# First token product of batch 1 in three round-format products, V rows for pairs 2 and 3, and a new list of the attention phase

## The chip, the cores and the metric

One core of a Trainium2 chip runs the whole program. The metric is the device time of one execution in microseconds (us), the median of the runs shown. Before the change it is 558.04 us (three runs, 557.51 to 558.55).

## The reference, cut to what matters

The program computes three blocks in a row on two batches of 768 rows and 512 columns.

```python
# attention: 8 heads of 64 columns, blocks of 32 rows, a window of 16
k_sum = k.reshape(B, H, nb, block, D).max(axis=3)
v_sum = v.reshape(B, H, nb, block, D).mean(axis=3)
scores = [local scores inside the window | scores on k_sum + log(block)]
x = softmax(scores) @ [v | v_sum]            # becomes (B, 768, 512)
# first mixer: across the rows (tokens), then across the columns (channels)
xt = x.transpose(0, 2, 1)
h = relu(xt @ w_tok1) @ w_tok2               # w_tok1 is 768 x 256
u = x + h.transpose(0, 2, 1)
y = u + relu(u @ w_ch1) @ w_ch2
# second mixer: normalised rows, channels only
out = y + relu(norm(y) * g @ moe2_w_ch1) @ moe2_w_ch2
```

## The kernel before, in words

**Two phases.** The first is the attention phase: attention of both batches, both token products of batch 0 and the first token product of batch 1. The order of every engine's instructions in it is written out by hand in the list FRONT: each word is a letter (what is done, by the table `do` in `attention`) and a number (which piece). The words are issued in that order on all engines, so each engine works through its own words strictly in turn, and waits where a word isn't ready. The second phase is the channel products, about 464 us of them, ordered by the planner and, later, by the program.

**Attention.** Two heads make a pair; pairs 0 to 3 are batch 0, 4 to 7 are batch 1. A pair has three groups n (n = 3 * pair, + 1, + 2), so there are 24. Each group goes through q (scores, TensorE, 16 small products), m (mask and minimum, VectorE), e (exponential, ScalarE), t (four transposes, TensorE), c (copy out, ScalarE), a (product with V, TensorE) and n (division by the row sum, VectorE), which writes the group into `u`. Keys, queries and V have three buffers each, by pair modulo 3, so a pair's loads wait for the last use of the pair three before.

**V.** There are two ways to get a pair's V in rows. Pairs below NT come transposed with their neighbours (v loads 552 KB into a wide tile), get their block means on VectorE or GpSimd (s or p, and S or T), and are turned by TensorE: w is four transposes, and x or X copies them out by ScalarE or VectorE. The other pairs load V rows ready from memory (r, 780 KB) and V transposed (v, 384 KB); GpSimd makes the means (s), TensorE turns them once (S, one transpose), ScalarE copies them out (z), and GpSimd writes them into the rows (u). NT is 4.

**Token products.** The weights arrive as 64-bit words in halves of 128 x 512 (h loads one, W and D decode it). Halves 0 to 2 are `w_tok1`. `g1(b, hf, t)` is a piece of the first token product: six F32 products of 128 x 256 accumulate over the six row tiles of a batch, then ScalarE makes the high half of the result (hh) and VectorE the low half (hl). There are eight pieces, four for each batch: g0 to g3 for batch 0, g10, g11, g20 and g21 for batch 1. `g2` is the second token product (six pieces g4 to g9 for batch 0); there each operand is split into a high half in the round format (F32R) and the rest, and `mm3` makes three products: high by high, high by low, low by high. C splits off the high half of a weight half (ScalarE), O the low half (VectorE). P, or g12 to g19, transpose `u` of batch 0 for the second phase.

**f** is a product of zeros on TensorE that nothing reads.

**Around the change.** The first token product of batch 1 needs all of `u` of batch 1, so its pieces g20 and g21 stand at the end of the list. The second phase's first product follows the last transposes.

Of the kernel before, what the change touches and what calls it, by code (L numbers as in the profile page):

```python
# [11 lines left out]
F32 = mybir.dt.float32  # L12
# [32 lines left out]
EARLY = 16  # L45
NEG = -8e9
EPS = 1e-9
NT = 4
FRONT = """
d0 f d1 f j0 f f j1 f f i0 v0 f i1 f l1 f K0 f v1 q0 l2 f f m0 f f e0 f h1 q1 t0 m1 f c0 f q2  # L50
e1 f m2 f l3 e2 t1 s0 f f f v2 t2 k1 S0 h2 w1 v3 w0 K1 x1 h0 q3 X0 c1 w2 m3 p1 a0 e3 q4 n0 c2 t3 m4
x2 a1 e4 k2 q5 T1 a2 n1 K2 c3 w3 m5 W1 t4 x3 D1 q6 c4 a3 e5 n2 w5 m6 w4 x5 t5 x4 n3 q7 p2 c5 k3 a4
e6 m7 a5 e7 t6 n4 r4 q8 n5 J3 S2 p3 t7 c6 m8 h4 w7 W2 y2 w6 X7 c7 q9 l4 e8 X6 a7 D2 v4 a6 S3 W0 v5
n7 w11 l5 w9 m9 x11 t8 x9 w8 D0 c8 q10 x8 w10 n6 e9 g1 X10 W4 k4 D4 K4 s4 t9 m10 C4 g0 c9 O4 G1 e10
H1 s5 q11 G0 H0 t10 l6 m11 S4 a8 e11 k5 q12 h3 z4 t11 c10 h7 n8 u4 a9 h5 m12 v7 e12 a10 n9 r5 J5 q13
n10 c11 t12 m13 a11 c12 k6 e13 q14 S5 a12 J6 m14 z5 e14 u5 t13 n12 q15 n11 c13 t14 W3 m15 a13 W7 D3
q16 e15 g2 m16 e16 s7 n13 D7 C3 c14 t15 O3 C7 q17 c15 t16 m17 G2 a14 e17 H2 q18 n14 r7 c16 a15 m18
e18 a16 l7 n15 q19 n16 W5 g3 h6 D5 v6 h8 m19 C5 h9 e19 r6 O5 t17 t18 G3 c17 q20 H3 k7 c18 g7 m20 K7
e20 g5 H7 W6 q21 H5 s6 g8 m21 e21 D6 S7 g6 W8 H8 h10 C6 D8 z7 t19 W9 u7 S6 g4 z6 O6 h11 H6 u6 q22 H4
g9 m22 e22 q23 H9 a18 m23 b g19 n18 g12 G19 a17 G12 H19 t20 H12 c19 g13 n17 c20 g16 t21 G16 a19 G13  # L60
H16 e23 a20 H13 n19 g11 c21 n20 t23 G11 g15 H11 t22 G15 g14 c22 H15 a21 G14 g18 c23 n21 a22 G18 H14
a23 n22 g10 n23 H18 g20 G10 H10 g21 G20 H20 P17 G21 G17 H21 H17
"""
SCALE = 1.0 / math.sqrt(D)

# [5 lines left out]
class Kern:  # L71
# [342 lines left out]
    def prep_v2(self, i):  # L414
        nc = self.nc
        if i < NT:
            zs = self.vs.pop(i)
            nc.scalar.activation(
                self.wide[i][:, :, 0:NB],
                zs.rearrange("p (o n) -> p o n", o=1).to_broadcast([P, 7, NB]),  # L420
                AF.Copy,
                scale=1.0 / BLOCK,
            )
            return
        self.psv = self.ps_pt.tile([P, 512], F32, tag="pt", name=f"psv{i}")
        nc.tensor.transpose(self.psv[:NK, 0:P], self.Z[i % 2], self.ident)

    def prep_v3(self, i):
        self.zs = self.att.tile([NK, P], F32, tag="zs", bufs=1, name=f"zs{i}")
        self.nc.scalar.activation(self.zs, self.psv[:NK, 0:P], AF.Copy, scale=1.0 / BLOCK)  # L430

    def prep_v4(self, i):
        nc, src = self.nc, self.zs
        V = self.V[i % 3].rearrange("p (w j) c -> p j w c", j=2)
        for a, j in ((0, 0), (96, 1)):
            out = V[a : a + NB, j, :, 0:130].rearrange("p w (r c) -> p w r c", r=2)[:, :, :, 0:64]
            x = src[a : a + NB].rearrange("p (o r c) -> p o r c", o=1, r=2).to_broadcast([NB, 6, 2, 64])
            nc.gpsimd.tensor_copy(out, x)

    def att_vtr(self, n):  # L440
        i, qd = divmod(n, 3)
        ps = self.ps_mm.tile([P, 512], F32, tag="mm", name=f"vtr{n}")
# [127 lines left out]

    def g1(self, b, hf, t):
        nc = self.nc
        ps = self.ps_mm.tile([P, 512], F32, tag="mm", name=f"g1_{b}_{hf}_{t}")
# [12 lines left out]
        yield  # L586
        nc.vector.scalar_tensor_tensor(hl, ps[:, :256], 0.0, f32(hh), op0=ALU.max, op1=ALU.subtract)
        yield

    def g2(self, b, only=None):  # L590
        nc = self.nc
        for st in range(ST) if only is None else (only,):
            ps = self.ps_mm.tile([P, 512], F32, tag="mm", name=f"g2_{b}_{st}")
# [19 lines left out]
    def transpose_u(self, g, only=None):  # L613
        nc = self.nc
        th, tl = self.new_xt(("u", g))
        for cc in range(CC) if only is None else (only,):
            ps = self.bank or self.ps_mm.tile([P, 512], F32, tag="mm", name=f"tu_{g}_{cc}")
            self.bank = None
            for j in range(GT):
                nc.tensor.transpose(  # L620
# [513 lines left out]
    def attention(self):  # L1134
# [8 lines left out]
        def other_bank(k):  # L1143
# [35 lines left out]
            "C": self.split_hi,  # L1179
            "O": lambda h: [0 for _ in self.split_lo(h)],  # L1180
# [15 lines left out]
    def run(self):  # L1196
# [260 lines left out]
```

## Time and profile before

| | |
|---|---|
| runs shown | 558.04 us median, 557.51 to 558.55 |
| the profiled execution's own time | 557.49 us |
| its span, first to last instruction | 555.7 us |
| TensorE busy | 548.7 us (99%), 3673 instructions |
| VectorE busy | 405.1 us (73%) |
| ScalarE busy | 272.2 us (49%) |
| GpSimd busy | 36.6 us (7%), all in the attention phase |
| memory traffic | 137 MB, 247 GB/s on average |

Busy TensorE is not TensorE at its peak: products are pipelined and their ends are modelled, so where work follows work the time of one is read from start to start. The profiled execution is 0.55 us faster than the median. Some records of products are missing, so counts are taken from the list and the code. The attention phase ends where the first channel product starts, at 91.3 us.

### The profile page before, as it was taken

The page shows a single profiled execution, that of the slowest core. Times are in us where ns is not written, and L with a number is a line of the kernel's source. Part 1 is how long each engine was busy: PE and PEld are TensorE (multiplying, and loading weights), DVE is VectorE, ACT ScalarE, POOL GpSimd, SP SyncE. Part 2 cuts the span into 40 slices and gives each one's busy share as a digit, 9 for nine tenths or more (in the row PEclk, how much of TensorE's full clock was granted, in tenths as well). Part 3 has the DMA queues.
Part 4 walks back from the last instruction along what each step waited for, and adds up shares of the span by engine and source line. Part 5 has one row for each costly group of instructions (what it writes and reads, how often), then busy time and mean ns, then how long its engine had stood idle before and what let it go on. Part 6 is the DMA issues. An engine that isn't in the chain of part 4 may idle for free.

```text
span 555.7 us, 10285 instructions
## 1 busy us (share of the span) xinstructions
PE 548.7 (99%) x3673; PEld 495.0 (89%) x3674; DVE 405.1 (73%) x977; ACT 272.2 (49%) x602; POOL 36.6 (7%) x76
## 2 busy tenths in 40 slices
PE   8999999999999999999999999999999999999997
PEld 4887789898998989989999988988989999999997
DVE  5989874648876887665579957888866776777771
ACT  5979663138755645454787325554422222334320
POOL 7454400000000000000000000000000000000000
PEclk9999999999999999999999999999999999999999
DMA  8876810435788779888656996898787897777455
GB/s 326 313 298 242 327 57 1 151 109 197 248 297 292 266 282 315 283 313 296 230 207 234 317 312 195 284 313 278 257 300 234 292 314 253 240 234 254 162 168 173
DMA packets 55651, 137.00 MB, mean 247 GB/s; under 512 B 5681, under 2 KB 13489, under 8 KB 55601
## 3 DMA queue, kind: packets, MB, share of 16 engines
q1 hardware_dynamic: 55600, 136.36, 71.6%
q8 instruction: 29, 0.48, 0.3%
q14 instruction: 22, 0.17, 0.1%
HBM read 101.73 MB, written 34.60 MB: 245 GB/s over the span
## 4 chain that ended last, share of the span: by engine, by line
PE 91%; ACT 3%; DVE 2%; DMA 2%; POOL 0%; issue 0%; SPq 0%; DVEq 0%; POOLq 0%; ACTq 0%
PE m L319 8%; PE m L318 8%; PE m L317 8%; PE acc_x L318 4%; PE acc_x L319 4%; PE acc_x L317 4%; PE g L575 3%; PE acc_y L319 2%; PE acc_y L318 2%; PE acc_y L317 2%; DMA V<-in_v_dram 2%; ACT pr L519 1%; PE av L547 1%; PE acc_m L319 1%; PE acc_m L318 1%; PE acc_m L317 1%
## 5 line engine op out<-in xcount | busy, mean ns | idle before, releaser
L317 PE MATMUL m<-slot,slot 128*128 128x384 f32 (+1 forms) x136 | 45.8, 337 | 0.0
L319 PE MATMUL m<-slot,slot 128*128 128x384 f32 (+1 forms) x136 | 45.4, 334 | 0.0
L318 PE MATMUL m<-slot,slot 128*128 128x384 f32 (+1 forms) x136 | 45.4, 334 | 0.0
L319 PE MATMUL acc_x<-slot,al 128*128 128x512 f32 x96 | 37.8, 394 | 0.0
L318 PE MATMUL acc_x<-slot,ah 128*128 128x512 f32 x96 | 37.8, 394 | 0.0
L317 PE MATMUL acc_x<-slot,ah 128*128 128x512 f32 x96 | 37.5, 391 | 0.0
L519 ACT ACTIVATE pr<-sn,mn 128x120 f32<-128x120 f32 x96 | 29.7, 389 | 6.6 <-DVE mn L504 6.6
L317 PEld LDWEIGHTS m<-slot,slot 128*128 128x128 f32 x136 | 25.6, 188 | 1.8
L318 PEld LDWEIGHTS m<-slot,slot 128*128 128x128 f32 x136 | 25.6, 188 | 1.6
L165 DVE SCALAR_TENSOR_TENSOR dec<-stage,dec 128x512 uint32<-128x512 uint32 x36 | 25.5, 708 | 0.7
L319 PEld LDWEIGHTS m<-slot,slot 128*128 128x128 f32 x136 | 25.5, 188 | 0.0
L142 ACT ACTIVATE dec<-stage 128x512 f32<-128x512 f32 x36 | 24.2, 676 | 0.1
L871 ACT ACTIVATE ah<-sm 128x384 fp32r<-128x384 f32 x16 | 8.4, 525 | 28.1 <-DVE sm L881 28.1
L575 PE MATMUL g<-u,tok 128*128 128x256 f32 x96 | 22.1, 383 | 0.0
L504 DVE CUSTOM_DVE_ANT_0 sn<-scores,mask 128x120 f32<-128x120 f32 x92 | 20.4, 277 | 2.2 <-PE scores L485 2.1
L703 ACT ACTIVATE f_B<-tx,gt 128x384 f32<-128x384 f32 x16 | 9.3, 582 | 25.4 <-PE tx L699 25.4
L319 PEld LDWEIGHTS acc_x<-slot,al 128*128 128x128 f32 x96 | 18.0, 188 | 4.0
L243 DVE TENSOR_TENSOR slot<-dec,slot 128x512 fp32r<-128x512 f32 x27 | 20.1, 743 | 0.1
L319 PE MATMUL acc_y<-slot,al_s 128*128 128x256 f32 x72 | 20.1, 280 | 0.0
L318 PE MATMUL acc_y<-slot,ah_s 128*128 128x256 f32 x72 | 20.1, 279 | 0.0
L575 PEld LDWEIGHTS g<-u,tok 128*128 128x128 f32 x96 | 17.8, 190 | 2.6 <-issue 0.3
L666 ACT ACTIVATE xn<-u,nb,rs 128x128 f32<-128x128 f32 x48 | 20.1, 483 | 0.0
(1516 smaller groups left out, 1732.5 us busy)
## 6 DMA issues: line engine op xcount, KB each, us to landing
stage<-in_wts_dram SPq DMA_DIRECT2D x62, 512.0 KB, 4.4
slot<-w1s SPq DMA_DIRECT2D x94, 256.0 KB, 3.6
w1s<-sps SPq DMA_DIRECT2D x16, 512.0 KB, 4.4
w2s<-sp SPq DMA_DIRECT2D x16, 512.0 KB, 3.4
slot<-w2s SPq DMA_DIRECT2D x16, 512.0 KB, 4.8
w2t<-wk SPq DMA_DIRECT2D x16, 512.0 KB, 5.0
slot<-w2t SPq DMA_DIRECT2D x8, 768.0 KB, 5.0
slot<-w2s SPq DMA_DIRECT2D x22, 256.0 KB, 4.3
```

The costliest lines, as they stand in the source:

```text
L142: fold = lambda out: nc.scalar.activation(out, high, AF.Prelu, scale=2.0**-112, alpha=-(2.0**32))
L165: put(m, t[:, :, 0], 29, m, op0=ALU.logical_shift_right, op1=ALU.bitwise_or)
L243: (engine or nc.vector).tensor_tensor(wl, x, f32(wh), op=ALU.subtract)
L317: nc.tensor.matmul(out, lhs[0], rhs[0], start=first, stop=False)
L318: nc.tensor.matmul(out, lhs[0], rhs[1], start=False, stop=False)
L319: nc.tensor.matmul(out, lhs[1], rhs[0], start=False, stop=last)
L504: nc.vector.tensor_tensor_reduce(sn[:, u], ps[u % 2][:, u // 2, :NK], self.mask[:, mv], scale=-SCALE, scalar=3e38, op0=ALU.add, op1=ALU.mi ...
L519: self.nc.scalar.activation(self.pr[n][:, u], sn[:, u], AF.Exp, bias=mn[:, u : u + 1], scale=-1.0)
L575: nc.tensor.matmul(ps[:, :256], self.tok1(st, t), self.u[:, b * ST + st, 256 * hf : 256 * hf + 256], start=st == 0, stop=st == ST - 1,)
L666: nc.scalar.activation(xn[:, j], self.u[:, g * GT + j, cc * P : cc * P + P], AF.Identity, bias=nb[:, j : j + 1], scale=rs[:, j : j + 1],)
L703: nc.scalar.activation(x, ps[:, :GN], AF.Copy, scale=self.gt[:, cc : cc + 1])
L871: nc.scalar.activation(ah, x, AF.Relu)
```

## The change

NT goes from 4 to 2, so pairs 2 and 3 get V rows from memory. Batch 1's first token product uses `mm3` on halves: `tok_hi` and `tok_lo` split the three halves of `w_tok1` (C0 to C2, O0 to O2), and `split_u` splits each group of batch 1 as it is ready (U12 to U23 on ScalarE, L12 to L23 on VectorE). The second pair of tiles for the parts takes the place of the third buffers of keys, queries and V, which B closes. The two accumulation banks of the attention phase are held as two fixed tiles used in turn. The list is a new one.

```diff
-NT = 4
+NT = 2
     def tok1(self, st, t):
         col = st * DTOK + t * P
-        return self.half[col // 512][:, col % 512 : col % 512 + P]
+        return self.tok[:, col // 512, col % 512 : col % 512 + P]
+    def tok_hi(self, h):
+        w, e = self.slot(h // 2), 512 * (h % 2)
+        self.half[h] = w[:, e : e + 512], w[:, 1024 + e : 1536 + e]
+        self.nc.scalar.copy(self.half[h][0], self.tok[:, h])
+    def tok_lo(self, h):
+        hi, lo = self.half[h]
+        self.nc.vector.tensor_tensor(lo, self.tok[:, h], f32(hi), op=ALU.subtract)
+    def u_parts(self, hf, qd):
+        return tuple(t[:, 2 * qd : 2 * qd + 2] for t in self.us[hf])
+    def parts_tiles(self, pool, hf):
+        self.us[hf] = [pool.tile([P, ST, 256], F32R, name=f"us{hf}{i}") for i in range(2)]
+    def close_late(self):
+        self.lctx.close()
+        self.parts_tiles(self.actx.enter_context(self.tc.tile_pool(name="parts", bufs=1, side="right")), 1)
+    def split_u(self, n, k):
...
+        hi, lo = (t[:, :, e : e + P] for t in self.u_parts(p // 2, qd))
+        x = self.u[:, b * ST + 2 * qd : b * ST + 2 * qd + 2, p * P : p * P + P]
+        if k == 0:
+            nc.scalar.copy(hi, x)
+        else:
+            nc.vector.tensor_tensor(lo, x, f32(hi), op=ALU.subtract)
+    def mm_bank(self, name):
+        if not self.banks:
+            return self.ps_mm.tile([P, 512], F32, tag="mm", name=name)
+        self.banks.rotate(1)
+        return self.banks[0]
     def g1(self, b, hf, t):
...
+            if b == 1:
+                rhs = tuple(x[:, st % 2] for x in self.u_parts(hf, st // 2))
+                self.mm3(ps[:, :256], self.weight(st // 2, st % 2 * DTOK + t * P), rhs, st == 0, st == ST - 1)
+                continue
```

Counted over the two lists, the words that differ in number are these; q, m, e, t, c, a, n, D, W, h, k and the pieces are as many as before (five more of the eight transposes of `u` are called P instead of g, which gives them a bank of their own).

| word | before | after | engine of one |
|---|---|---|---|
| f | 22 | 2 | TensorE |
| w (four transposes of V) | 12 | 6 | TensorE |
| x, X (copies of these) | 8, 4 | 5, 1 | ScalarE, VectorE |
| S as a copy / as one transpose | 3 / 4 | 0 / 6 | ScalarE / TensorE |
| z, u | 4, 4 | 6, 6 | ScalarE, GpSimd |
| s on VectorE / on GpSimd | 1 / 4 | 1 / 6 | |
| p (means of a wide tile) / T (their copy) | 3 / 1 | 1 / 2 | GpSimd |
| r (load of V rows) | 4 | 6 | DMA |
| B (closes the third buffers) | 0 | 1 | |
| K / J (copy of the key maxima) | 5 / 3 | 7 / 1 | ScalarE / GpSimd |
| C | 5 | 8 | ScalarE |
| O / o (low half of a weight half) | 4 / 0 | 3 / 4 | VectorE / GpSimd |
| U, L | 0, 0 | 12, 12 | ScalarE, VectorE |

The beginning and the end of the two lists:

```
before: d0 f d1 f j0 f f j1 f f i0 v0 f i1 f l1 f K0 f v1 q0 l2 f f m0 f f e0 f h1 q1 t0 m1 f c0 f q2 ...
... t23 G11 g15 H11 t22 G15 g14 c22 H15 a21 G14 g18 c23 n21 a22 G18 H14 a23 n22 g10 n23 H18 g20 G10 H10 g21 G20 H20 P17 G21 G17 H21 H17
after: d0 d1 f j0 j1 v0 l1 i0 v1 i1 l2 K0 q0 h0 v2 q1 m0 e0 f m1 q2 e1 s0 t0 l3 t1 c0 T0 k1 r2 w0 h2 m2 w2 K1 x0 v3 e2 h1 q3 a0 ...
... P12 L16 c22 g8 n21 W9 L17 G12 n20 U18 t23 H8 U20 g11 c23 L19 L18 H12 L20 D8 a23 G11 U21 a22 n23 h10
g10 n22 U23 H11 U22 L23 L21 L22 P16 P18 g20 G18 G10 H10 g21 G20 G16 H20 H16 H18 P17 P19 G17 G19 H17 G21 H21 H19
```

## Rows read from the trace of the kernel before

**Rows 1.** Windows: busy us per engine (instructions), clock, DMA share, GB/s; the second phase.
```profile
91.25:555.70 464.45, 461.21 (x2583) 427.20 (x2581) 333.82 (x674) 209.27 (x431) 0.00 (x0) 1.00 0.74 248
```

**Rows 2.** Windows: the attention phase from its first scores, in four stretches.
```profile
5.40:30.59 25.19, 24.82 (x400) 18.93 (x402) 21.30 (x109) 22.32 (x63) 12.54 (x26) 1.00 0.91 351
30.59:54.10 23.51, 22.79 (x344) 18.32 (x342) 21.72 (x104) 19.88 (x59) 11.92 (x21) 1.00 0.66 249
54.10:71.70 17.60, 16.30 (x146) 12.25 (x142) 15.88 (x54) 10.79 (x31) 7.77 (x14) 1.00 0.80 306
71.70:91.25 19.55, 19.55 (x206) 17.00 (x200) 9.92 (x34) 8.16 (x21) 0.00 (x0) 1.00 0.09 29
```

**Rows 3.** Waits of TensorE that show: who waited for whom, us, times, longest.
```profile
PE g L317 <- DVE u L604: 0.9, 1, 0.9
PE scores L485 <- POOL V L438: 0.5, 1, 0.5
```

**Rows 4.** Timeline of TensorE (start, us, line, operation): start of the program.
```profile
1.25 4.07 PE L1194 MATMUL warm_ps<-warm 128*128 128x512 bf16 x10 [1.25 <-DVE warm L1247]
5.40 0.64 PE L485 MATMUL scores<-K,Q 64*64 64x120 f32 x16
5.98 1.25 PE L1194 MATMUL warm_ps<-warm 128*128 128x512 bf16 x5
```

**Rows 5.** Timeline of TensorE: one of each of the attention phase's pieces.
```profile
30.10 0.65 PE L446 MATMUL vtr<-ident,VW 128*120 128x128 f32 x4
30.59 2.76 PE L575 MATMUL g<-u,tok 128*128 128x256 f32 x12
33.18 0.60 PE L528 MATMUL pt<-ident,pr 128*120 128x128 f32 x4
...
36.30 0.64 PE L485 MATMUL scores<-K,Q 64*64 64x120 f32 x16
36.87 0.65 PE L528 MATMUL pt<-ident,pr 128*120 128x128 f32 x4
37.36 0.27 PE L426 MATMUL psv<-ident,Z 128*120 128x128 f32 x1
37.56 0.69 PE L547 MATMUL av<-V,PT 121*64 121x65 f32 x16
38.18 0.64 PE L485 MATMUL scores<-K,Q 64*64 64x120 f32 x16
...
59.74 0.39 PE L317 MATMUL g<-hh,slot 128*128 128x512 f32 x1
59.97 0.39 PE L318 MATMUL g<-hl,slot 128*128 128x512 f32 x1
```

**Rows 6.** Timeline of TensorE near the end: round-format products of 256 columns.
```profile
536.20 0.28 PE L317 MATMUL acc_m<-slot 128*128 128x256 f32 x1
...
536.56 0.28 PE L317 MATMUL acc_m<-slot 128*128 128x256 f32 x1
```

**Rows 7.** Groups by line: count, busy us, mean ns of one, idle before.
```profile
L230 ACT CAST sp<-dec 128x256 fp32r<-128x256 f32 x8 | 3.2, 403 | 0.0
L222 ACT CAST slot<-dec 128x512 fp32r<-128x512 f32 x27 | 16.6, 614 | 2.1 <-DVE dec L165 2.1
L257 DVE TENSOR_TENSOR sp<-dec,sp 128x256 fp32r<-128x256 f32 x8 | 3.3, 416 | 0.0
L243 DVE TENSOR_TENSOR slot<-dec,slot 128x512 fp32r<-128x512 f32 x27 | 20.1, 743 | 0.1
L453 DVE COPY V<-vtr 120x512 f32<-120x512 f32 x4 | 2.7, 688 | 0.9 <-PE vtr L446 0.9
```

**Rows 8.** Timeline of all engines: VectorE's subtraction beside GpSimd's additions.
```profile
33.71 2.82 POOL L400 TENSOR_TENSOR VT<-VT 128x384 f32<-128x384 f32 x4 [7.90 <-DMA VT<-in_vt_dram]
...
34.12 1.14 DVE L243 TENSOR_TENSOR slot<-dec,slot 128x512 fp32r<-128x512 f32 x1
```

**Rows 9.** DMA issues of the first 92 us: KB each, median us to landing.
```profile
V<-in_v_dram SPq DMA_DIRECT2D x4, 780.0 KB, 7.0
```

More of the change, by code (lines that the diff above doesn't have):

```diff
@@ L47 @@
 EPS = 1e-9
-NT = 4
+NT = 2
 FRONT = """
[L50 to L59, printed above, removed]
@@ L60 @@
-g9 m22 e22 q23 H9 a18 m23 b g19 n18 g12 G19 a17 G12 H19 t20 H12 c19 g13 n17 c20 g16 t21 G16 a19 G13
-H16 e23 a20 H13 n19 g11 c21 n20 t23 G11 g15 H11 t22 G15 g14 c22 H15 a21 G14 g18 c23 n21 a22 G18 H14
-a23 n22 g10 n23 H18 g20 G10 H10 g21 G20 H20 P17 G21 G17 H21 H17
+d0 d1 f j0 j1 v0 l1 i0 v1 i1 l2 K0 q0 h0 v2 q1 m0 e0 f m1 q2 e1 s0 t0 l3 t1 c0 T0 k1 r2 w0 h2 m2 w2
+K1 x0 v3 e2 h1 q3 a0 p1 m3 c1 e3 n0 q4 w1 m4 t2 x1 k2 x2 q5 T1 e4 a1 m5 l4 J2 w3 c2 n1 q6 e5 s2 t3
+m6 w4 e6 X3 q7 a2 m7 c3 t4 x4 n2 q8 c4 k3 W0 S2 w5 e7 a3 m8 a4 D0 K3 t5 z2 x5 u2 q9 c5 n3 h4 t6 e8
@@ new lines @@
+m9 v4 a5 r3 n4 q10 l5 c6 s3 n5 W2 a6 m10 W1 t7 t8 c7 n6 q11 c8 D1 e9 v5 a8 a7 D2 e10 S3 t9 n7 g1 h5
+z3 k4 r4 c9 h3 m11 K4 l6 W4 D4 r5 t10 G1 u3 e11 q12 g0 m12 C0 e12 n8 s4 k5 c10 K5 q13 C4 a9 m13 e13
+t11 o4 v6 n9 t12 q14 H1 c11 s5 G0 a10 m14 W5 l7 a11 c12 n10 q15 n11 t13 S4 H0 g2 z4 D5 c13 v7 u4 e14
+h7 m15 h6 W3 C5 t14 D3 S5 e15 o5 q16 a13 m16 G2 a12 C3 n13 q17 o3 H2 U13 g3 k6 z5 c14 e16 u5 m17 n12
+L13 t15 s6 G3 t16 K6 H3 c15 k7 q18 e17 a15 m18 a14 e18 n15 q19 s7 r7 n14 g7 U15 r6 m19 h8 e19 q20 H7
@@ new lines @@
+U14 t17 m20 K7 g6 C2 c16 O0 W7 L15 t18 L14 C1 q21 D7 c17 a16 e20 a17 m21 h9 S7 g5 H6 z7 U12 u7 c18
+n17 W6 n16 g4 e21 D6 S6 t19 H4 z6 h11 U16 u6 q22 c19 y2 H5 t20 C7 m22 b g15 e22 P13 O2 a19 G15 a18
+O1 G13 q23 H15 c20 n18 g9 W8 H13 U17 C6 n19 g14 H9 o6 B U19 t21 G14 t22 m23 c21 a20 e23 H14 a21 L12
+P12 L16 c22 g8 n21 W9 L17 G12 n20 U18 t23 H8 U20 g11 c23 L19 L18 H12 L20 D8 a23 G11 U21 a22 n23 h10
+g10 n22 U23 H11 U22 L23 L21 L22 P16 P18 g20 G18 G10 H10 g21 G20 G16 H20 H16 H18 P17 P19 G17 G19 H17
@@ L63 @@
+G21 H21 H19
 """
@@ L424, in prep_v2 @@
             return
-        self.psv = self.ps_pt.tile([P, 512], F32, tag="pt", name=f"psv{i}")
-        nc.tensor.transpose(self.psv[:NK, 0:P], self.Z[i % 2], self.ident)
+        self.psv[i] = self.ps_pt.tile([P, 512], F32, tag="pt", name=f"psv{i}")
+        nc.tensor.transpose(self.psv[i][:NK, 0:P], self.Z[i % 2], self.ident)
     def prep_v3(self, i):
-        self.zs = self.att.tile([NK, P], F32, tag="zs", bufs=1, name=f"zs{i}")
-        self.nc.scalar.activation(self.zs, self.psv[:NK, 0:P], AF.Copy, scale=1.0 / BLOCK)
+        self.zs[i] = self.att.tile([NK, P], F32, tag="zs", bufs=1, name=f"zs{i}")
+        self.nc.scalar.activation(self.zs[i], self.psv.pop(i)[:NK, 0:P], AF.Copy, scale=1.0 / BLOCK)
     def prep_v4(self, i):
-        nc, src = self.nc, self.zs
+        nc, src = self.nc, self.zs.pop(i)
         V = self.V[i % 3].rearrange("p (w j) c -> p j w c", j=2)
@@ L441, in att_vtr @@
         i, qd = divmod(n, 3)
-        ps = self.ps_mm.tile([P, 512], F32, tag="mm", name=f"vtr{n}")
+        ps = self.mm_bank(f"vtr{n}")
         for u in range(4):
@@ L572, in g1 @@
         nc = self.nc
-        ps = self.ps_mm.tile([P, 512], F32, tag="mm", name=f"g1_{b}_{hf}_{t}")
+        ps = self.mm_bank(f"g1_{b}_{hf}_{t}")
         for st in range(ST):
+            if b == 1:
+                rhs = tuple(x[:, st % 2] for x in self.u_parts(hf, st // 2))
+                self.mm3(ps[:, :256], self.weight(st // 2, st % 2 * DTOK + t * P), rhs, st == 0, st == ST - 1)
+                continue
             nc.tensor.matmul(
@@ L592, in g2 @@
         for st in range(ST) if only is None else (only,):
-            ps = self.ps_mm.tile([P, 512], F32, tag="mm", name=f"g2_{b}_{st}")
+            ps = self.mm_bank(f"g2_{b}_{st}")
             for t in range(2):
@@ L616, in transpose_u @@
         for cc in range(CC) if only is None else (only,):
-            ps = self.bank or self.ps_mm.tile([P, 512], F32, tag="mm", name=f"tu_{g}_{cc}")
+            ps = self.bank or self.mm_bank(f"tu_{g}_{cc}")
             self.bank = None
@@ L1178, in attention @@
             "b": lambda _: self.close_wide(),
-            "C": self.split_hi,
-            "O": lambda h: [0 for _ in self.split_lo(h)],
+            "C": lambda h: (self.split_hi if h > 2 else self.tok_hi)(h),
+            "O": lambda h: [0 for _ in self.split_lo(h)] if h > 2 else self.tok_lo(h),
+            "B": lambda _: self.close_late(),
+            "U": lambda n: self.split_u(n, 0),
+            "L": lambda n: self.split_u(n, 1),
             "o": lambda h: [0 for _ in self.split_lo(h, nc.gpsimd)],
@@ L1230, in run @@
         att = self.att
-        self.Q = [att.tile([P, S], F32, name=f"Q{i}") for i in range(3)]
-        self.K = [att.tile([P, 7, 184], F32, name=f"K{i}") for i in range(3)]
+        self.us = {}
+        self.parts_tiles(att, 0)
+        self.actx, self.lctx = actx, ExitStack()
+        late = self.lctx.enter_context(tc.tile_pool(name="late", bufs=1, side="right"))
+        at = (att, att, late)
+        self.Q = [at[i].tile([P, S], F32, name=f"Q{i}") for i in range(3)]
+        self.K = [at[i].tile([P, 7, 184], F32, name=f"K{i}") for i in range(3)]
         self.PT = [att.tile([NK + 1, 512], F32, name=f"PT{i}") for i in range(2)]
-        self.V = [att.tile([P, NW, VC], F32, name=f"V{i}") for i in range(3)]
+        self.V = [at[i].tile([P, NW, VC], F32, name=f"V{i}") for i in range(3)]
         self.VT = [att.tile([P, S], F32, name=f"VT{i}") for i in range(2)]
-        self.vs, self.vps, self.sn = {}, {}, {}
+        self.vs, self.vps, self.sn, self.psv, self.zs = {}, {}, {}, {}, {}
         self.Z = [att.tile([P, NK], F32, name=f"Z{i}") for i in range(2)]
@@ L1263, in run @@
         nc.scalar.activation(first, first, AF.Exp)
-        self.wps = self.ps_mm.tile([P, 512], F32, tag="mm", name="warm_ps")
+        self.banks = deque(self.ps_mm.tile([P, 512], F32, tag="mm", name=f"mm{i}") for i in range(2))
+        self.wps = self.banks[0]
         E = mybir.EngineType
@@ L1268, in run @@
             self.attention()
+        self.banks = None
         actx.close()
```

4 lines of the change are left out of this document (added).

## The prediction, as put on record

> **What bounds the kernel now.** I read the windows by phase first. In the second phase TensorE is busy 461.21 of 464.45 us [rows 1], so nothing else sets its length; the change leaves its work alone, and whatever the attention phase gains or loses should arrive at the end one for one. Then the attention phase by stretches [rows 2]. The first scores start at 5.40 us [rows 4] and the phase ends at 91.25, so 85.85 us count. The reader is to see that three engines share the load: VectorE is busy 21.30, 21.72 and 15.88 us in the first three stretches, 58.9 of 66.3 us or 89%, ScalarE 22.32 of 25.19 in the first, and only in the last 19.55 us are both half idle. TensorE's own waits that show are few, 0.9 us for VectorE's additions and 0.5 us for GpSimd's writes into V [rows 3]; but its busy time is padded by modelled ends, so I rebuild its work from start to start.
>
> Of one piece [rows 5]: scores 0.57 us (36.30 to 36.87), four transposes 0.49 (36.87 to 37.36), one transpose of means 0.20, the product with V 0.62 (37.56 to 38.18), four V transposes 0.49 (30.10 to 30.59), an F32 piece of the first token product 2.59 (30.59 to 33.18), one round-format product of 512 columns 0.23. Over the list: 24 x (0.57 + 0.49 + 0.62) = 40.3; 12 w at 0.49 = 5.9; 4 S at 0.20 = 0.8; 8 pieces at 2.59 = 20.7; 36 products of g2 at 0.23 = 8.3; 24 transposes of `u` at a quarter of 0.49 = 2.9. That is 78.9 us, without the fills: 92% of the 85.85 us. TensorE is the bound, with 7 us of waits (some filled by f) that come from the other two engines being nearly full.
>
> **The change part by part.** *Token product.* A piece of batch 1 goes from six F32 products to 18 round-format ones of 256 columns. These stand in the trace of the tail at 0.12 us each, weights loaded anew each time (536.20 to 536.56 for three, [rows 6]): 18 x 0.12 = 2.16 against 2.59, so 0.43 saved, four times: -1.7 us. The saving is small because three products replace what costs as much as 3.6.
>
> *V rows.* Six w go: 6 x 0.49 = -2.9 us. Two more S come: +0.4. TensorE together: -4.2 us, to 74.7.
>
> *Fills.* Ten of the 22 run before the first scores and the rest in waits, so they save nothing. They cost what they did for the clock. The fills of the first 4 us take 4.07 us for ten, 0.41 each, and five later ones 1.25, 0.25 each [rows 4]: 512 columns at about 1.2 and 2.4 GHz, whatever the granted clock of 1.00 in that window says. In the new list one fill stands before the first scores. So the first products run at the low level. Below, this costs nothing (the path goes on through VectorE and ScalarE); above, all that is done until the level rises is done at twice the time, with no row for when. I take the first scores alone as on the path, since the first group's mask waits for them: +0.57 us. The Trainium skill, "TensorE: Matmul & The Clock Gate", Part 1 (the HAM clock gate), says that throttled is the default state and activity releases it. The two prices of the fills agree; by that rule the removal of the fills speaks against the change, and what it would do is the first rival below.
>
> *ScalarE.* Twelve U of 256 columns at 0.40 and three C of 512 at 0.61 [rows 7] add 6.7 us; fewer V copies give some back. VectorE: six L before the last pair (6 x 0.42 = 2.5) and three O (3 x 0.74 = 2.2) against four O moved to GpSimd (-3.0) and three X dropped (3 x 0.69 = -2.1): -0.3 us up to there, and six L (2.5 us) in the last stretch, where VectorE has 9.6 us idle [rows 2]. Cover for both is that idle time and ScalarE's 6.8 idle us in the third stretch; if it is gone, their terms enter in full (second rival). The last six groups' splits stand before g20. Behind the last a of the list, TensorE has g10 (2.16) and two transposes of `u` (6 x 0.12 = 0.7), 2.9 us, while VectorE has two n, H11, and three L; at 0.42 a piece, and an n estimated at 0.6 (one of 0.42 and a short one), about 2.9 us too. I price the wait of g20 at 0, with +0.9 as its upper end and nothing as its lower, since g20 has no earlier place.
>
> *GpSimd.* Two more pairs by s, u and four o. Its subtraction has no row; its nearest run, four additions of 384 columns and fewer, takes 2.82 us [rows 8], so an o lies between VectorE's 0.74 and 2.8. I take 1.4, half the run. It is idle for 54 of 91 us, and no word of TensorE stands close behind an o. What it does to VectorE is dearer: the subtraction that met GpSimd's additions took 1.14 us [rows 8] against a mean of 0.74 [rows 7]. The Trainium skill, "SBUF — State Buffer", Who interferes with whom, says that a VectorE instruction with two SBUF inputs contends with a GpSimd instruction that reads SBUF, and that the second to issue waits until the first is done. The row agrees in sign. Every L, O and o is of that kind, so by the rule the second rival is where the new words go.
>
> *Loads.* For pairs 2 and 3, 780 + 384 KB come in place of 552: 1.2 MB more. In the first stretch the DMA share is already 0.91 at 351 GB/s [rows 2], so 1.2 MB are 3.5 us of it. Below: nothing, since the third buffer is free from the start for pair 2 and the weights' halves can come later (share 0.09 in the last stretch). Above: 3.5 us. I take 0.
>
> *The third buffers and the two fixed banks.* B closes buffers whose last use is pair 5, before the first U of the last pairs; the banks are used in turn as before. Each could hold TensorE up to one evacuation (0.6 us) or give as much; I take 0.
>
> *Sum.* 74.7 us of work at the same 92% is 81.2 us in place of 85.85: -4.6. With the clock's +0.57, -4.1 us. I keep the 92% because the first two stretches already show three engines loaded alike (20 to 25 us in each), and in the new list the loads in front of the last pairs stay alike. The profiled execution's own 557.49 becomes 553.4; the median of the runs shown is 0.55 above it, so 553.9.
>
> **The rivals.** *The low clock stays (slower).* Place: the first stretch. Price: each us of full-speed work done at the low level takes one more; the 8% of waits there (2 us of 25.19) absorb a little, and the gain of 4.6 us is used up when 6.6 us of work have run low, that is if the level rises later than about 5.4 + 13 = 19 us. Low until 30.59 it is 12.6 us of work, so 12.6 - 2.0 - 4.6 = +6 us: 564.0. For: the first groups leave gaps. Against: at half speed TensorE would have twice the work in the same time and be busy without gaps, and with the few fills of the later list words the scores at 36.30 are at 0.57 [rows 5]. Chance 0.08.
>
> *VectorE becomes the bound.* If VectorE keeps 89% in the first three stretches, and half of the nine new two-input words there meet GpSimd at 1.14 - 0.74 = 0.4 each, they add 1.8 - 0.3 = 1.5 us, 1.7 at 89%; TensorE's savings are then waits, except the two pieces of the last stretch (-0.9). +0.8: 558.8; with none meeting, 556.8. For: its 92% of 23.51 us in the second stretch. Against: four o off VectorE. Chance 0.12.
>
> *V rows come late.* 1.2 MB in a stretch with 9% room: 0.91 x 25.19 + 3.5 = 26.4 us, at least 1.2 more than it has, at most 3.5; V takes 7.0 us from issue to landing [rows 9]. Middle 2.4: 556.3. Against: halves of weights can yield. Chance 0.08.
>
> *The list also packs better.* If the shown and hidden waits are halved (96% of the time), 74.7 / 0.96 = 77.8: -8.0 + 0.6 = -7.4, 550.6. For: six fewer copies and four o that leave VectorE where it held TensorE up [rows 3]. Against: the splits that come. Chance 0.13.
>
> **How the numbers follow.** The forecast has 0.59, its own range 551.5 to 556.0 (the clock's term up to 2.7 for the first three scores and two transposes at double time, the tail's wait 0.9, the loads' lower end, and up to 2.4 us of better packing). With the rivals, 8 times in 10 it lies in 550.0 to 558.0: below are half of the packing case, above most of the clock's and over half of VectorE's. A measurement of this kernel tells 0.2% (1.1 us) from nothing. Faster: 0.58 of the forecast, 0.13 packing, 0.06 of V rows, 0.02 of VectorE, 0.79. Slower: 0.07 of the clock, 0.04 of VectorE, 0.11. Same: the remaining 0.10.
>
> **What would show it.** Right: no group of V transposes after pair 1; pieces of batch 1 at 2.2 us; the first channel product near 87.2 us, the second phase within 0.5 us of 464.3 us; the first scores at 0.9 us or more, and 0.57 again by the time groups 3 to 5 run. Wrong: scores still over 0.9 us at 19 us (clock); VectorE over 92% busy and TensorE waiting for L or n (second rival); TensorE or GpSimd waiting for V loads of pairs 2 and 3 (third); TensorE waiting before g20 by more than 0.9 us.

## The result, and the profile after

The changed kernel takes 550.31 us (median of four runs, 549.64 to 551.12) against 557.77 us of the kernel before, measured beside it: ratio 0.9865, 95% interval 0.9846 to 0.9884. That is 7.5 us less. The forecast was 553.9. The direction was right and the range of 8 in 10 (550.0 to 558.0) holds the time, but it lies below the forecast's own range (551.5 to 556.0), and the gain is nearly twice what was forecast: the rival "the list also packs better" (550.6) has the number that came. The profiled execution took 550.67 us (span 549.0) and lies 0.36 us above its median, where that of before lay 0.55 below its own; 0.9 us of the miss on the median is this.

The windows of the changed kernel, for the same phases and stretches as [rows 1, 2]: the first row is the second phase, the next four the attention phase from its first scores (busy us with instruction counts for TensorE, its weight loads, VectorE, ScalarE, GpSimd, then granted clock, DMA share, GB/s).

```profile
84.58:549.00 464.42, 461.16 (x2583) 427.12 (x2581) 334.20 (x675) 209.37 (x432) 0.00 (x0) 1.00 0.74 248
5.17:30.79 25.62, 24.11 (x404) 18.88 (x404) 20.94 (x115) 21.77 (x63) 14.82 (x28) 1.00 0.99 389
30.79:52.10 21.31, 21.26 (x272) 17.52 (x270) 18.97 (x84) 17.92 (x53) 16.61 (x23) 1.00 0.89 358
52.10:66.70 14.60, 14.53 (x212) 11.55 (x208) 13.86 (x62) 13.89 (x42) 7.28 (x15) 1.00 0.62 219
66.70:84.58 17.88, 17.88 (x198) 16.64 (x195) 14.57 (x46) 10.25 (x27) 1.28 (x1) 1.00 0.17 61
```

The second phase is as long as before (464.42 and 464.45). Everything came from the attention phase, which ends at 84.58 instead of 91.25. The first token piece starts at 30.79, where before it started at 30.59, so the time was gained behind that point. There TensorE has almost no idle time left: 53.67 us busy of 53.79, where before it had 58.63 of 60.66. The words on either side of the point are not the same in the two lists, so I count them by pieces, at the prediction's prices. Behind it stand 57.4 us of work before and 54.0 after: 1.7 less for the token product, and one group's scores, transposes and product with V (1.7) that now stand ahead. The waits behind it therefore fell from 3.2 us (60.66 - 57.4) to nothing (53.79 - 54.0; the prices are 0.2 too high there). Ahead of it stand 21.5 us of work before and 20.7 after, so the waits there rose from 3.7 us (25.19 - 21.5) to 5.0 (25.62 - 20.7): six w are gone, and nothing was won there. The two rows of the stretch behind, before and after:

```profile
30.59:91.25 60.66, 58.63 (x685) 47.57 (x684) 47.52 (x189) 38.83 (x108) 19.69 (x34) 1.00 0.52 195
```

```profile
30.79:84.58 53.79, 53.67 (x674) 45.71 (x673) 47.40 (x190) 42.06 (x119) 25.17 (x38) 1.00 0.58 222
```

VectorE is busy for the same 47.5 us in a stretch 6.9 us shorter, ScalarE for 3.2 us more and GpSimd for 5.5 more. The three other engines got fuller and TensorE stopped waiting for them there.

TensorE's timeline of the changed kernel (start, us, line, operation), for what [rows 4 to 6] showed of before: the first scores, the start of the first F32 token piece, the first and last product of one round-format piece, and the first channel product.

```profile
5.17 1.08 PE L524 MATMUL scores<-K,Q 64*64 64x120 f32 x16 [3.32 <-ACT K L412]
...
12.01 0.64 PE L524 MATMUL scores<-K,Q 64*64 64x120 f32 x16
30.79 2.75 PE L618 MATMUL mm<-u,tok 128*128 128x256 f32 x12
...
73.37 0.36 PE L350 MATMUL mm<-us,slot 128*128 128x256 f32 x1
...
75.49 0.28 PE L352 MATMUL mm<-us,slot 128*128 128x256 f32 x1
...
84.58 0.42 PE L350 MATMUL g_('u', 0)_3_1596<-xt,slot 128*128 128x384 f32 x1
```

The piece is 18 products from 73.37 to 75.49 and 0.12 more, 2.24 us with its first product 0.08 longer than the rest; 2.16 was predicted. The first scores run at the low level (1.08 us) and are back at 0.64 by 12.01. The changed kernel's own waits of TensorE, which answer to [rows 3] (who waited for whom: us, times, longest):

```profile
PE scores L524 <- ACT K L412: 3.3, 1, 3.3
...
PE scores L524 <- DVE mn L543: 0.5, 1, 0.5
```

The first is the start of the program. No wait of TensorE for V, for a load of pairs 2 and 3 or for a split is among them. GpSimd does wait for such a load, from 29.7 to 32.6 us, for the V rows of pair 3 (word u3):

```profile
POOL V L477 <- DMA V<-in_v_dram: 2.9, 1, 2.9
```

That is a sign that the prediction named for its rival of late V rows. It holds up no word of TensorE, which is idle for 0.12 us in all behind 30.79. The changed kernel's groups of the new words and of the copies of V, which answer to [rows 7] (count, busy us, mean ns, idle before):

```profile
L244 POOL TENSOR_TENSOR slot<-dec,slot 128x512 fp32r<-128x512 f32 x4 | 5.5, 1378 | 4.8 <-issue 3.5 <-ACT slot L223 1.2
L342 DVE TENSOR_TENSOR us<-u,us 128x256 fp32r<-128x256 f32 x12 | 4.7, 426 | 0.0
L492 ACT COPY V<-mm 120x512 f32<-120x512 f32 x5 | 2.8, 585 | 0.7 <-PE mm L485 0.7
```

Each new word costs what was taken for it: an o on GpSimd 1.378 us (1.4), an L 0.426 (0.42); the twelve U on ScalarE take 0.403 each (0.40). The 1.4 was half the run of another instruction, so that it fits this well is in part luck. The size of the words was not where the forecast was off; what they free and what holds TensorE was.

**Where TensorE had waited.** The chain of waits shows it better than the busy times. Between 62 and 71 us the chain of the kernel before lies off TensorE for 8.6 us (start, us, what):

```profile
61.97 0.61 PE scores L485 x16
...
63.51 0.67 DVE dec L160
64.20 0.68 DVE dec L165
64.89 0.68 DVE u L604
...
65.94 1.29 DVE dec L165
67.23 1.09 DVE slot L243
68.39 1.27 DVE u L604 x2
...
71.18 0.64 PE scores L485 x16
```

VectorE decodes weight halves, splits one and divides groups one after another, and the next scores wait behind it. TensorE is not idle for all of that time: it is busy for 7.30 of the 8.60 us, and the waits that show are the 0.9 us of [rows 3] and 0.4 us for the mask's minimum (row L485 <- DVE mn of the same view, which [rows 3] leaves out). The chain of the changed kernel stays on TensorE from 30.95 us, but for one stretch of about 1 us at 40.3 and this one of 2.6 us:

```profile
47.95 2.80 PE mm L618 x12
50.78 0.39 ACT hh L628
51.20 0.42 DVE hl L630
51.62 0.86 DVE ks L403
...
53.34 0.64 PE scores L524 x16
```

### The profile page after: what moved, and what is told of

Same layout as the page of the kernel before. It is cut to its first block, busy times and chain, and to the rows that moved or that the text cites. A ratio compares the mean times of both kernels' runs of the same rounds, so it can differ in the third digit from the quotient of the medians.

```text
span 549.0 us, 10290 instructions
## 1 busy us (share of the span) xinstructions
PE 539.6 (98%) x3656; PEld 491.8 (90%) x3656; DVE 404.9 (74%) x985; ACT 275.0 (50%) x615; POOL 44.2 (8%) x82
## 4 chain that ended last, share of the span: by engine, by line
PE 95%; DVE 2%; ACT 1%; DMA 1%; issue 0%; SPq 0%; ACTq 0%; DVEq 0%
PE m L352 8%; PE m L351 8%; PE m L350 8%; PE acc_x L351 4%; PE acc_x L352 4%; PE acc_x L350 4%; PE acc_y L352 2%; PE acc_y L351 2%; PE acc_y L350 2%; PE mm L618 2%; PE pt L567 2%; PE scores L524 2%; PE av L586 2%; PE mm L350 1%; PE acc_m L352 1%; PE acc_m L350 1%
## 5 line engine op out<-in xcount | busy, mean ns | idle before, releaser
L352 PE MATMUL acc_x<-slot,al 128*128 128x512 f32 x96 | 37.8, 394 | 0.0
L351 PE MATMUL acc_x<-slot,ah 128*128 128x512 f32 x96 | 37.8, 394 | 0.0
L558 ACT ACTIVATE pr<-sn,mn 128x120 f32<-128x120 f32 x96 | 29.7, 390 | 2.2 <-DVE mn L543 2.2
L166 DVE SCALAR_TENSOR_TENSOR dec<-stage,dec 128x512 uint32<-128x512 uint32 x36 | 25.9, 721 | 0.7
L170 DVE SCALAR_TENSOR_TENSOR dec<-stage,dec 128x512 uint32<-128x512 uint32 x23 | 15.9, 690 | 6.9 <-ACT stage L143 6.7
L351 PE MATMUL acc_y<-slot,ah_s 128*128 128x256 f32 x72 | 20.1, 279 | 0.0
L350 PE MATMUL acc_y<-slot,ah_s 128*128 128x256 f32 x72 | 20.0, 278 | 0.0
L524 PE MATMUL scores<-K,Q 64*64 64x120 f32 x368 | 15.6, 287 | 4.3 <-ACT K L412 3.3
```

What stands on the lines that cost most here:

```text
L166: put(m, t[:, :, 0], 29, m, op0=ALU.logical_shift_right, op1=ALU.bitwise_or)
L170: put(m, t[:, :, 1], 3, m, op0=ALU.logical_shift_left, op1=ALU.bitwise_or)
L350: nc.tensor.matmul(out, lhs[0], rhs[0], start=first, stop=False)
L351: nc.tensor.matmul(out, lhs[0], rhs[1], start=False, stop=False)
L352: nc.tensor.matmul(out, lhs[1], rhs[0], start=False, stop=last)
L524: nc.tensor.matmul(ps[j][cols, e, :NK], Q[rows, 64 * w : 64 * w + 64], K.rearrange("p v c -> p (v c)")[rows, a : a + NK], start=True, stop ...
```

## The experiments

Ratios stand against the kernel before, run beside each version on the same chip; where two of them are compared, the difference is taken in ratios, times 557.9 us, and its interval is the root of the squared half-widths. The theory after the result: TensorE's own work fell by the 4.2 us predicted, and the rest of the gain is order, above all words moved off VectorE. Its rival: the two parts each bring more than TensorE's work shows.

### e1_f32_token and e2_splits_unread: the token product undone

```diff
-            if b == 1:
+            if b == 1 and TOK3:      # TOK3 = False: six F32 products as before
e1: also without the words C0 to C2, O0 to O2, U12 to U23, L12 to L23
e2: with all of them, nothing reads what they make
```

> The changed kernel with batch 1's first token product in F32 again and all its splits (U, L, C0 to C2, O0 to O2) left out; V rows and the order of the rest stay. Work theory (time follows the work taken off TensorE): four pieces go back from 2.16 to 2.59 us, +1.7, so 552.0 against 550.3 for the changed kernel. Rival, the splits crowd ScalarE and VectorE: taking out 6.7 us of ScalarE and 7.2 us of VectorE gives at least as much back, 550.3 or less.

> The changed kernel with F32 products for batch 1's first token product, while all splits are still made and nothing reads them. With e1_f32_token (552.5, no splits) it tells what the splits cost. Splits hidden: 552.0 to 552.5, as e1. Splits crowd ScalarE and VectorE: 553.5 or more.

e1: 552.46 us, ratio 0.9897 (0.9881 to 0.9912), 1.8 us behind the changed kernel, give or take 1.4. The 1.7 us predicted (four times 0.43) fits, and so does the stretch from the first token piece to the first channel product: 55.42 us in e1 for 53.79. e2: 552.15 us, 0.9898 (0.9884 to 0.9913), the same as e1 (give or take 1.2), and the same stretch takes 55.54. So the thirty words that split the operands cost nothing that can be measured in the new list, where VectorE and ScalarE have room at the end.

### e9_new_wide and e12_new_wide_ahead: the V rows undone in the new list

```diff
-NT = 2
+NT = 4
 for pairs 2 and 3 the words r, s, S, z, u go; p, T, w6 to w11 and their copies x come
e9: w9 to w11 between the first two token pieces    e12: w9 w10 x9 x10 w11 x11 ahead of both
```

> The changed kernel with NT 4 again: pairs 2 and 3 from wide tiles, their means by GpSimd (p, T), six w and six copies on ScalarE where z and u of these pairs stood; round-format token product and order of the rest as changed. Work theory: +2.5 us of TensorE, 552.8. Waits theory: the six copies (3.5 us) on a ScalarE that is nearly full in front of the last pairs add to it, 554 or more. V-rows rival (loads cost as much as w): 550.3.

> As e9 (the changed kernel with pairs 2 and 3 from wide tiles, 555.5), but with pair 3's w9 to w11 and their copies set in one block ahead of the first piece of the token product instead of between its pieces, where the two shared banks made them wait for each other and where, in e9 and e10, one of them overwrote that piece's sums before they were read. If e9's loss beyond the work of six w (2.5 us) came from the shared banks: 553 or less. If V rows are worth more than TensorE's work, because ScalarE's copies fill the stretch: 554.5 or more.

e9: 555.52 us, 0.9959 (0.9947 to 0.9972). In it w10 writes into the bank of a token piece of batch 0 before ScalarE and VectorE read that piece, so these instructions run on other data than the reference's. e12 has no such overlap: 554.46 us, 0.9937 (0.9923 to 0.9950), 4.0 us behind the changed kernel, give or take 1.3, where 2.5 was predicted; that is at the edge of the second of its two expectations (554.5 or more). e9's placing costs 1.2 us more than e12's, give or take 1.0. The two stretches of e12 (its first scores start at 5.34), ahead of its first token piece and behind it, show where they lie:

```profile
5.17:34.34 29.17, 26.70 (x426) 21.06 (x426) 23.50 (x117) 25.09 (x69) 18.65 (x35) 1.00 0.93 357
34.34:88.26 53.92, 53.80 (x674) 45.81 (x673) 45.59 (x189) 41.93 (x117) 20.44 (x30) 1.00 0.52 190
```

All of it is ahead of the first token piece, 29.0 us from its first scores against 25.62. TensorE is busy 2.59 us longer there (26.70 and 24.11), which fits the predicted 2.5, and idle 0.8 us longer (2.30 and 1.51). Single profiles can't tell these two shares more closely: with the same words in this stretch as the changed kernel, e1, e2 and e3 take 26.99, 24.45 and 24.83 us, with TensorE busy for 24.91, 23.19 and 23.56. ScalarE has 3.3 us more to do in it: the copies of V that the rows save. From 13 us on, the chain of the changed kernel holds no such copy; e12's holds five, three of them from 25 us on:

```profile
25.77 0.89 ACT V L494 x2
...
33.24 0.56 ACT V L494
```

Their group in e12:

```profile
L494 ACT COPY V<-mm 120x512 f32<-120x512 f32 x11 | 6.1, 586 | 0.7 <-PE mm L487 0.5
```

Eleven in e12, five in the changed kernel, 3.3 us; the kernel before had eight of them on ScalarE and four on VectorE, so e12 loads ScalarE more than the kernel before did. The prediction said that "fewer V copies give some back" on ScalarE and priced that at nothing.

### e10_new_list_old_parts: the new list with both parts undone

```diff
+NT = 4 and TOK3 = False; the words of e9, without C0 to C2, O0 to O2, U, L
```

> The new list with both parts undone: F32 token product without splits, pairs 2 and 3 from wide tiles as in e9; low halves o3 to o6 stay on GpSimd. What is left of the change is the order. Work theory: order worth nothing, 557.8 (4.2 us more than 550.3 and the 3.3 of it that I had not foreseen lost as well). Waits theory: the order alone takes about 3 us, 554.5.

556.08 us, 0.9967 (0.9955 to 0.9980), with the same overwritten piece as e9. Neither expectation holds: it lies in the middle between them. The new list without the parts, with two fills for 22, four o for O and some copies on other engines, brings 1.8 us, give or take 0.7. With F32 products the V rows are worth 3.9 us (e10 to e1), with wide V the token product only 0.4 us (e10 to e9; give or take 1.0), and with V rows 1.8 (e1 to the changed kernel; give or take 1.4). These intervals overlap, so it isn't shown that the parts help each other. e10 has e9's placing of w9 to w11; if that costs 1.2 us here too, the list is worth 3.0 and the V rows 2.7, but no run has F32 products with e12's placing.

### e3_o_on_vector: the four subtractions back on VectorE

```diff
-... t11 o4 v6 ... e15 o5 q16 ... q17 o3 H2 ... H9 o6 B ...
+... t11 O4 v6 ... e15 O5 q16 ... q17 O3 H2 ... H9 O6 B ...
```

> The changed kernel with the four low halves o3 to o6 on VectorE (O) instead of GpSimd, at the same places. Work theory: VectorE has room, +0 to +0.5, 550.3 to 550.8. Waits theory (the extra gain over my forecast came from VectorE's relief): four times 0.74 us return to a nearly full VectorE in front of the last pairs, +2 to +3, 552.5 to 553.5. If GpSimd's readings were what slows VectorE, it would be faster, 549.5 or less.

551.59 us, 0.9890 (0.9876 to 0.9903): 1.4 us slower than the changed kernel, give or take 1.3, the smallest step that these runs tell from nothing. It lies between the two theories' ranges, above the one and below the other. Its profile says why. The chain of e3 from 37.8 to 54.4 us lies on VectorE again, as it did before the change:

```profile
42.56 0.41 DVE hl L631
...
43.34 1.33 DVE dec L167
...
45.94 0.69 DVE dec L167
46.63 0.60 DVE slot L245
...
54.41 0.64 PE scores L525 x16
```

TensorE waits four times for the mask's minimum, as this row of e3's waits says, and once in the changed kernel (0.5 us) and in the kernel before (0.4). Behind the first token piece it is idle for 1.17 us in e3, for 0.12 in the changed kernel:

```profile
PE scores L525 <- DVE mn L544: 1.6, 4, 0.5
```

These rows also show a price. The same decoding takes 0.69 us alone and 1.33 while GpSimd copies into V (43.31 to 45.37), and e3's first O takes 1.21 beside GpSimd's additions for the means (38.29 to 41.12) where an O takes 0.74 on average [rows 7]. The Trainium skill, "SBUF — State Buffer", Who interferes with whom, says that a VectorE instruction with two SBUF inputs contends with a GpSimd instruction that reads SBUF, and that the one that issues later waits for the other to end; delays of 0.5 to 0.6 us, less than one of GpSimd's instructions here (2.83 us for four, 2.06 for two), agree in size.

### e4_fills and e5_old_few_fills: the clock at the start

```diff
e4, new list:  -d0 d1 f j0 ... q0 h0     +d0 d1 f f f f f f f f f j0 ... q0 f f h0
e5, old list:  20 of the 22 f taken out
```

> The changed kernel with eight more fills before the first scores and two between the first and second, so that TensorE's clock is up when the attention starts, as in the kernel before. My forecast's term: the first scores alone are on the path, 1.08 back to 0.64 or so, -0.5, 549.8. If all work at the low level is on the path (scores three times, transposes four times two pieces): about -2, 548.3. If the wait for the loads covers it all: 550.3, no change.

> The kernel before with its 22 fills cut to two, at the places that they have in the new list. My forecast's term: +0.6, 558.4. If the level stays low for longer because the old list's groups leave gaps: +2 or more, 560 or above. If the first groups wait for loads and for ScalarE anyway: no change, 557.8.

e4: 549.97 us, 0.9859 (0.9846 to 0.9873), 0.3 us below the changed kernel, with an interval of 1.3 on either side. e5: 558.01 us, 1.0005 (0.9996 to 1.0013), 0.3 us, between -0.2 and +0.7. Both leave open whether the forecast's term or none is right, and rule out the 2 us. The timelines do show the level of the first scores. First e4, with nine fills in the first 4.6 us, then e5 with one:

```profile
5.70 0.64 PE L526 MATMUL scores<-K,Q 64*64 64x120 f32 x16 [1.06 <-ACT K L414]
```

```profile
5.53 1.08 PE L486 MATMUL scores<-K,Q 64*64 64x120 f32 x16 [3.67 <-DMA Q<-in_q_dram]
```

In e4's profile the first token piece starts at 30.16 and the first channel product at 83.96, both 0.6 us ahead of the changed kernel (30.79, 84.58). But e2 has the changed kernel's words up to that piece, without more fills, and starts it as early, here e4 and then e2:

```profile
30.16 2.75 PE L620 MATMUL mm<-u,tok 128*128 128x256 f32 x12
```

```profile
30.07 2.75 PE L619 MATMUL mm<-u,tok 128*128 128x256 f32 x12
```

e3 and e1, with these words too, start it at 30.53 and 32.29. So the 0.6 us are within what differs from one execution to the next, and neither the profiles nor the medians tell the predicted 0.57 from nothing. What is settled is the rival: a low level up to 30.59 would by the prediction's price have cost some 10 us (12.6 - 2.0), and it doesn't.

### e6_old_vrows and e11_old_vrows_later: the V rows in the old list

```diff
-NT = 4
+NT = 2
e6:  r2 after l3, r3 before a2; s2 s3 for p2 p3; z2 u2, z3 u3; w6 to w11 and their copies out
e11: h0 and h2 ahead of r2, r3 behind a4, s3 behind s2
```

> V rows alone: the old list with NT 2, pairs 2 and 3 loading V rows (r2 after l3, r3 after a2), their means by s, S, z and u, without w6 to w11 and their copies; fills and F32 token product as before. Work theory: six w less, two S more, -2.5 us against 557.8, so 555.3. Waits theory: the old list's stretch that VectorE bounds comes later than these pairs and eats a part, 556 to 557. V-rows rival: the loads come late, 557.8 or more.

> V rows alone in the old list once more (e6 took 563.2), now with the weights' halves h0 and h2 loaded ahead of r2, r3 loaded behind a4, and the means of pair 3 made right behind those of pair 2. If e6 lost by the order of the loads and of the means: 555.5 to 557. If V rows don't fit the old list whatever the place of the loads: 560 or more.

e6: 563.20 us, 1.0090 (1.0076 to 1.0103), 5 us slower than before, with less to do on TensorE. e11: 564.80 us, 1.0114 (1.0096 to 1.0132). All four versions with the old list (e6 to e8, e11) are the changed kernel's program with that list, so they also have its two fixed banks and B. Ahead of the first token piece this costs nothing: there e7 has the old list's words unchanged and takes 25.19 us, as the kernel before does. Behind it no run tells it apart. Three windows of e6, and then the first two of them in the kernel before:

```profile
25.00:30.00 5.00, 2.58 (x52) 2.02 (x52) 4.16 (x18) 2.83 (x8) 4.33 (x7) 1.00 0.98 372
30.00:35.00 5.00, 2.76 (x24) 2.11 (x25) 3.19 (x6) 3.07 (x9) 3.21 (x6) 0.73 0.94 344
35.00:40.00 5.00, 5.00 (x17) 4.01 (x16) 2.68 (x11) 1.27 (x3) 4.53 (x9) 0.58 0.22 89
```

```profile
25.00:30.00 5.00, 4.88 (x88) 4.13 (x86) 4.74 (x20) 4.83 (x13) 0.66 (x3) 1.00 0.99 364
30.00:35.00 5.00, 5.00 (x35) 4.39 (x28) 4.93 (x16) 3.95 (x12) 1.21 (x2) 1.00 0.99 396
```

The DMA engines are full in both, but from 20 to 25 us they are half idle in the kernel before (share 0.52) and full in e6 (0.99), which carries 1.2 MB more in front of what is needed next. TensorE waits for GpSimd's means, whose chain goes back to a load of transposed V of 10.4 us that lands at 21.4, and for a decoded weight half, and is busy for 2.58 and 2.76 of 5 us; the granted clock falls to 0.73 and then, with TensorE busy throughout, to 0.58. One token piece, the first, runs at 1.2 GHz:

```profile
PE psv L466 <- POOL Z L443: 2.3, 1, 2.3
PE mm L619 <- DVE tok L168: 1.8, 1, 1.8
```

```profile
33.58 5.49 PE L619 MATMUL mm<-u,tok 128*128 128x256 f32 x12 [1.81 <-DVE tok L168]
```

It starts 3.0 us later than before (30.59) and takes 2.7 us longer (5.28 from its start to the next word's, at 38.86, for 2.59): 5.7 of the 6.3 us by which e6's first channel product is late (97.53 and 91.25). These are two of the prediction's rivals, the late rows and the low clock, in one place and in the other list. That the clock falls after gaps in which TensorE waits for loads is what the Trainium skill, "TensorE: Matmul & The Clock Gate", HAM oscillation, describes; this trace agrees, with gaps that go back to a load by way of GpSimd. e11 had r3 later and the weights earlier, and TensorE is half idle at the same place (busy 2.65 of 5 us from 25 to 30, the granted clock 0.66 in the next 5 us). Its waits there are for GpSimd's writes into V (1.1 us), for a copy of key maxima by GpSimd (1.0) and for a decoded weight half (1.0), so moving these loads did not help, and what would have is open.

### e7_old_token and e8_old_both: the token product, and both parts, in the old list

```diff
e7: `if b == 1:` with mm3, C0 to C2, O0 to O2, U and L each put in as its group is ready; NT = 4
e8: the words of e6 and e7 together, NT = 2
```

> The token product alone: the old list with NT 4, batch 1's first token product in three round-format products, C0 to C2 and O0 to O2 set beside a14 to a16 and each U and L a few words behind its n. Work theory: 4 x 0.43 = 1.7 us less, 556.1. Waits theory: the three O (2.2 us) and the first L come into the stretch in which VectorE is the bound, 557.8 or more.

> Both parts in the old list with its fills, without the new order. Work theory: -4.2, 553.6, and the new order brings the other 3.3 us of the change. If the order brings nothing: 550.3. If the order brings nearly all, since the old order cannot use the freed time: 556 or more.

e7: 561.27 us, 1.0061 (1.0048 to 1.0074), 3.4 us slower than before. One window of e7, and the same of the kernel before:

```profile
50.00:60.00 10.00, 7.84 (x120) 6.30 (x119) 9.40 (x33) 8.00 (x21) 5.58 (x8) 1.00 0.66 247
```

```profile
50.00:60.00 10.00, 9.46 (x142) 7.73 (x142) 8.87 (x41) 7.80 (x22) 4.80 (x8) 1.00 0.70 262
```

The third busy time of the row, VectorE's, rises from 8.87 to 9.40 us (e7 has 9.2 or more in every ten from 40 to 80), and TensorE's falls by 1.6. In this window TensorE waits for GpSimd's means for 1.5 us and for a division for 0.6, and elsewhere in the phase for the mask's minimum, 2.3 us. e7's chain here lies on VectorE and ScalarE, and two of the new O stand in it:

```profile
54.10 0.94 DVE slot L321
...
58.24 0.69 DVE slot L321
```

This fits the prediction's second rival, VectorE as the bound, which the new list avoids.

e8: 566.03 us, 1.0147 (1.0133 to 1.0161). The losses of e6 and e7 add up (0.90% and 0.61%, 1.51% together). From here to the changed kernel nothing differs but the list (the order, the fills, the four o, a few copies on another engine, the bank of five transposes of `u`), and it is worth 15.7 us.

## Why the prediction was right and where it was not

**What bounds the kernel, and that the second phase stands still.** Right: 464.42 us against 464.45, and every microsecond of the attention phase arrived at the end.

**TensorE's work.** Right, in its parts too, as far as the runs tell. A round-format piece is 2.24 us for 2.16; e1 puts the token product at 1.8 us for 1.7 (give or take 1.4); e12's busy time puts the V rows' work at 2.59 us for 2.5, in a stretch that differs by 1.7 us of busy time between profiles of the same words. By the prediction's prices the whole is 74.7 us of pieces from the first scores at 5.17 to 84.58.

**"74.7 us of work at the same 92%".** This step failed. The work takes 79.41 us, 94%, where the step gave 81.2. Its reason was that the first two stretches show three engines loaded alike, so their loads in front of the last pairs would hold TensorE up as before. One share for the whole phase also hid where the waits lay: ahead of the first token piece TensorE's work is 85% of the time before and 81% after, behind it 95% and all of it. The runs show two things in place of the step. Words that left are ones TensorE had waited for: four subtractions moved to GpSimd are worth 1.4 us, give or take 1.3, and take 1.05 us of idle time with them (e3); the V rows are worth 4.0 us, give or take 1.3, for 2.5 of TensorE's work, with ScalarE's copies of V in the chain of the version without them (e12). Taken out of the changed kernel one at a time, the token product (1.8), the V rows (4.0) and the four o (1.4) come to 7.2 of the 7.5 us, though such shares need not add up, as the old list shows. And a busy engine does not hold TensorE up as such: VectorE is 95% busy from 52.1 to 66.7 us in the changed kernel, more than in any stretch of [rows 2], and TensorE is busy 14.53 of 14.60 us beside it. In e3 and e7, with VectorE busy for 98% (37.7 to 54.4 us) and 92 to 97%, TensorE does wait. That what counts is whether the word that TensorE needs stands behind others fits all of this, but it is argued: no run moves a word without changing the load too. A share of waits belongs to an order, and I carried it from one order to another.

**The clock's +0.57.** Neither shown nor refuted: the medians (e4 0.3 us, with 1.3 on either side; e5 0.3, from -0.2 to +0.7) can't tell it from nothing, and the profiles of the same words differ by more. The first scores at 1.08 us and 0.64 by 12.01 are as forecast.

**The terms at nothing.** The wait of g20 is none: from 66.70 to 84.58 TensorE is busy throughout. The loads show in no wait of TensorE in the new list, at a DMA share of 0.99 and 389 GB/s in the first stretch [rows 2: 0.91 and 351], though GpSimd waits 2.9 us for pair 3's rows; whether they are part of the 1.3 us by which the waits ahead of the first token piece rose isn't shown. In the old list the version with the same loads loses 5 us (e6). The splits cost nothing that can be measured (e2). The third buffers and the fixed banks show in no wait of TensorE.

**The rivals.** VectorE as the bound does not happen in the new list; late V rows happen there to GpSimd, for 2.9 us, and not to TensorE. In the old list both fit what the traces show. Better packing had the reasons that proved true, "six fewer copies and four o that leave VectorE", and stood at 0.13 because the splits were set against them, which e2 shows to cost nothing that can be measured. From the same two reasons the forecast could have taken part of the packing. That the rival's 550.6 lies so near is in part luck: it had the waits halved, and by its own count they fell from 7 us to 4.7.

**Added up.** The forecast for the first channel product was 87.2, the trace has 84.58. Of these 2.6 us, 0.2 are the first scores at 5.17 for 5.40, 1.8 the 94% for 92%, and 0.6 the clock's term, counted on top in the forecast, while whatever the clock cost is inside the 79.41 us of the trace.

**What stays open.** Each part loses in the old list as I put it in; I did not look for the best places, so it isn't shown that the old list could not have taken them with smaller moves. No run has the old list with the fixed banks alone. Which of the new list's many moves carry the 15.7 us beyond the o is open too. No version ran clearly below the changed kernel; e4 with its fills is 0.3 us lower, which the runs can't tell from nothing.

## What to carry to other kernels

Where four engines in turn each stand near 90%, price a change by the words that the bounding engine has to wait for, not by busy shares: find in the chain of waits which words stand there, and see whether the change takes them away or puts more in front. Removing work can pay more than its own time if it leaves that chain (4.0 us for 2.5 in e12), and loads or splits that look free can cost several us if they enter it (5.0 in e6, 3.4 in e7, where a gain was expected). A share of waits for a whole phase hides where the waits are: count work and time on either side of a fixed point. A part that loses in the order it was put into isn't thereby a bad part: both parts here lose 0.6% and 0.9% alone and gain with an order made for them.

## What was not expected of the hardware

In e6 the granted clock fell to 0.73 and 0.58 in the middle of the attention phase (30 to 35 and 35 to 40 us) after TensorE had been busy for only 2.58 of 5 us, and in e11 to 0.66 after 2.65 of 5. In e6 the token piece behind the gap took 5.28 us for 2.59, so there the gap was paid about twice: once as a wait and once at 1.2 GHz after it. VectorE's two-input words take 1.21 us (the subtraction) and 1.33 us (the decoding with its integer shift) beside GpSimd in e3, and 0.69 us each without it; the prediction had the subtraction's delay, not the decoding's. Four executions with the same words up to the first token piece (the changed kernel, e1, e2, e3) took 24.45 to 26.99 us for them, while the stretch behind it took 53.79 us in the changed kernel and 53.80 in e4, whose words there are the same.
